# A chunked attention with two feed-forward layers on one core: another order of stores, preparation steps and low halves

## The chip, the cores and the metric

The kernel runs on one core of one Trainium2 chip. The metric is the device time of one execution in microseconds, the median of the runs. The core has TensorE (products; its weight loads are shown apart), VectorE (DVE), ScalarE (ACT), GpSimd (POOL) and SyncE (SP). In this kernel all DMAs are issued by SP, one after the other. Each engine takes its instructions in the order in which they are written; across engines only semaphores hold an instruction back.

## The reference

Attention within chunks of 64 tokens, 8 batches, 8 heads, 576 tokens, 64 columns a head; its output, 4608 tokens by 512, goes through two feed-forward layers with 2048 hidden columns:

```
scores = scale * q_c @ k_c^T ; attn = softmax(scores) ; x = attn @ v_c
h = x @ w_in1 ; g = h * sigmoid(1.702 h)               ; x = g @ w_out1
h = x @ w_in2 ; g = max(h, 0) + alpha * min(h, 0)      ; out = g @ w_out2
```

All arrays are float32 to the reader, but the weights arrive as 64-bit floats, so the kernel reads them as words and builds the 32-bit value from them ("decoding").

## The kernel before

**Precision.** A float32 factor is split into a high half (a cast by ScalarE to the type that TensorE multiplies fast) and a low half (the value minus the high half, a subtraction by VectorE or GpSimd). A product is three passes: high x high, low x high, high x low. Twelve matmuls of 128x512 are one such product of a tile.

**The plain stage.** The 4608 tokens are nine blocks of 512. The first five go through layer 1 in the plain form. For each block and each of 16 slices f of the hidden columns, `emit_h` makes 12 matmuls into `psH` (L652), ScalarE the activation and its high half, VectorE the low half `gs`, and `emit_y` 12 matmuls into `psY` (L682). One such pair is two *half slots*; there are 160. In the first block the weights are loaded, decoded (VectorE, L186 to L202) and split (`split_w`, high half by ScalarE L151, low half L154) as they are first needed.

Into the half slots a table puts everything else, as functions on a group of 128 tokens or on a step (`put(when, fn, g)`; `half_slot(k)` runs what is due). [...] Scores, maximum, exponential and normalization follow, and `att_PV` (L593) multiplies with the values that `load_v` brought. TensorE's `att_PV` reads what the fetch brings. For the first groups the buffer `off` is the one that also holds the scores `e`, read by the products of L558.

**Two kinds of preparation.** The last four blocks of layer 1, and all of layer 2, are computed by *pairs* of blocks with seven instead of eight products on quarters (Strassen and Winograd's scheme). It needs sums of quarters of the weights. For layer 1, 32 `fold` steps add them up on GpSimd from the weights that are in memory and store them (`wi<-fold`, `wo<-fold`). For layer 2, 32 *preparation steps* each load raw weights (`prep_load`, 2 DMAs), take the absolute value (`prep_abs`, ScalarE L183), decode (`prep_decode`, VectorE, 4 operations), make the sums (GpSimd, 4 operations, L293), cast two high halves (`hi`, ScalarE L283), subtract two low halves (GpSimd L285) and store all four (`wi<-g`, `wi<-u`, `wi<-sums`; `prep_store_a` and `prep_store_b`). 19 of these steps are in the plain stage, 13 in the first two pairs. A DMA that stores is queued by `send_later` and issued by `send_due` at the start of the next half slot, before that half slot's loads and swaps; the results `ysb` of a block are issued at once.

**The pairs.** A pair is four groups of 14 `h_item` (L903, six matmuls) and 7 `y_item` (L1051, twelve). A counter `clock` goes up by one for each `h_item` and by two for each `y_item`; `at(when, fn)` puts work at a value of it. Of the operands of the second product, GpSimd makes differences (`diff`, L984), ScalarE the high half (`op_hi`, L974) and VectorE the low half (`op_lo`, L979); in the first two pairs the loaded weights are split as well (`split_factor`, high L822, low L823 by GpSimd for `wi`, VectorE for `wo`). The first two pairs are layer 1's (`p < N1`), the other five layer 2's.

Of the kernel before, what the change touches and what calls it, by code (L numbers as in the profile page):

```python
# [36 lines left out]
TAU = (4, 10, 16, 22) + tuple(28 + 4 * i for i in range(28))  # L37
QK_T_AT = {4: 18, 5: 24}
QK_AT = {2: 3, 3: 9}
END = (4, 8)  # L40
PREP_AT = tuple(30 + 6 * i for i in range(19))
FOLD_AT = tuple(33 + 7 * i // 2 for i in range(32))
LATE_AT = (4, 20, 36, 52, 68, 84, 98)
# [26 lines left out]
def tile_chunk_attention_two_ffn(  # L70
# [185 lines left out]
    def send_later(**dma):  # L256
        waiting.append((half + 1, dma))

    def send_due():
        while waiting and waiting[0][0] <= half:  # L260
            nc.sync.dma_start(**waiting.pop(0)[1])

    def prep_store(step, lo, hi, ts):
        kind, j, m = step
        dst = wi2[j][:, lo:hi, m] if kind == "wi" else wo2[j // 2][:, lo:hi, j % 2, m]
        for a, t in enumerate(ts):
            (late.get("send") or send_later)(out=dst[:, :, a], in_=t)
# [40 lines left out]
    def fold(step):  # L308
# [17 lines left out]
        send_later(out=dst, in_=u)  # L326
# [80 lines left out]
    def off_copy(k):  # L407
        off_t[k] = off_p.tile([P, DW + PW], F32, tag="off", name="off")
# [9 lines left out]
    def off_fetch(k):  # L418
        t, o = ops_t[k], off_t.pop(k)
# [157 lines left out]
    def att_PV(g):  # L577
# [35 lines left out]
        if blk >= NPL:  # L613
            send_later(out=x1d[blk][:, :, i * P:(i + 1) * P], in_=xg)
# [7 lines left out]
    def split_x(j):  # L622
# [6 lines left out]
        for c in range(KT):  # L629
            nc.vector.tensor_tensor(  # L630
# [44 lines left out]
    def emit_y(n):  # L675
# [10 lines left out]
        if f == NF - 1:  # L686
            if j < NPL - 1:
                sbs = x_p.tile([P, 4, 512], F32, tag="x", name="ysb")
            for t, ps in enumerate(y_t.pop(j)):
# [8 lines left out]
                nc.sync.dma_start(out=x2d[j][:, t], in_=sb)  # L698
# [155 lines left out]
    def second_layer():  # L854
# [134 lines left out]
        def plan_group(p, gr, u):  # L989
# [6 lines left out]
            }.get((p, gr), (27, 30, 34, 36, 44, 46, 49))  # L996
            for i, nm, hi in zip(
# [7 lines left out]
                (p, gr), (24, 32, 29, 38)  # L1005
# [8 lines left out]
        def plan_late(p, u):  # L1014
            for when in LATE_AT:
# [9 lines left out]
        def plan_pair(p, u):  # L1025
# [154 lines left out]
    with tc.manual_schedule():  # L1180
# [72 lines left out]
        for i, g in enumerate(GROUP_ORDER):  # L1253
            t = TAU[i]
            if i < GPB:
                for fn, at in ((att_T, -3), (att_X, 1), (att_N, 2), (att_AT, 5), (att_PV, 6)):
                    if i > 0 or fn is not att_T:
                        put(t + at, fn, g)
                if i > 1:
                    put(QK_AT[i], partial(load_qkv, names="qk"), g)  # L1260
                if i == 0:
                    put(t, att_S_matmuls, g)
                put(t + 7, load_v, GROUP_ORDER[i + 1])
                continue
            pv = TAU[i + LAG] if i + LAG <= last else TAU[last] + END[i + LAG - last - 1]
            before = QK_T_AT.get(i, TAU[i - LAG] + 1)
            put(before - LEAD, load_nat, g)
            put(before, qk_T, g)
# [24 lines left out]
        for n in range(NPL * NF):  # L1293
# [72 lines left out]
        assert not between  # L1366
# [35 lines left out]
```

## Time and profile before

| what | us |
|---|---|
| median of 3 runs (1626.81 to 1630.45) | 1629.92 |
| the profiled execution, of which all rows here are | 1631.56 |
| its span, first to last instruction | 1629.8 |
| TensorE busy | 1550.8 |
| VectorE, ScalarE, GpSimd busy | 1218.5, 973.0, 739.8 |

The share of busy time is an average over stages. The plain stage lasts to about 543 us, the first two pairs to about 920 us, the rest is layer 2's pairs. The granted clock is the share of the full TensorE clock that the chip granted in a stretch: 1.00 is 2.4 GHz, 0.50 is 1.2 GHz.

### The profile page before, as it was taken

The numbers are of one execution on the slowest core, as the hardware profiler recorded it, in microseconds if no ns is written. First come the engines' busy times: TensorE is split into PE (matmuls) and PEld (weight loads), VectorE is DVE, ScalarE is ACT, GpSimd is POOL, SyncE is SP. The second block draws the span as 40 slices with busy tenths as digits, with TensorE's granted clock in tenths as the row PEclk, the third lists the DMA queues.
The fourth block names the chain that finished last, engine by engine and source line by source line (L and its number), as shares of the span: only waits on it lengthen the run. The fifth ranks groups of instructions, "written<-read, shape, count | busy, mean of one in ns | idle before, by whom it ended". The sixth has DMA issues, their size and how long they took to land.

```text
span 1629.8 us, 25569 instructions
## 1 busy us (share of the span) xinstructions
PE 1550.8 (95%) x9167; PEld 1293.0 (79%) x9169; DVE 1218.5 (75%) x1379; ACT 973.0 (60%) x1393; POOL 739.8 (45%) x637
## 2 busy tenths in 40 slices
PE   8998998999989988989899999999999999999998
PEld 5776786877778867767677788888888888999998
DVE  7988776676674547888778966887788778868767
ACT  6767665665564465656655665656565655656653
POOL 0003655646564187878878225332532342143330
PEclk9999999999999999999999999999999999999999
DMA  9914778787787264546645577669766966898984
GB/s 250 322 44 130 209 214 233 199 237 213 214 227 211 75 192 136 152 125 189 190 133 148 177 237 241 193 186 271 224 187 193 274 204 203 213 360 255 261 269 143
DMA packets 414223, 331.51 MB, mean 203 GB/s; under 512 B 138512, under 2 KB 348560, under 8 KB 414096
## 3 DMA queue, kind: packets, MB, share of 16 engines
q1 hardware_dynamic: 414096, 329.87, 69.2%
q8 instruction: 73, 1.20, 0.3%
q14 instruction: 54, 0.44, 0.1%
HBM read 251.67 MB, written 67.11 MB: 196 GB/s over the span
## 4 chain that ended last, share of the span: by engine, by line
PE 55%; DVE 9%; issue 5%; DMA 4%; POOL 4%; ACT 3%; SPq 1%; POOLq 0%; DVEq 0%; ACTq 0%
PE psYa L1051 14%; PE psHa L903 13%; PE psYb L1051 10%; PE psHb L903 9%; PE psY L682 5%; PE psH L652 4%; POOL u L293 1%; POOL u L285 1%; DMA wi2t<-wi 1%; DVE o L979 1%; DVE u L197 1%; DVE yacc L1089 1%; DMA w<-wo 1%; DVE xop L799 1%; DMA ops<-off 1%
## 5 line engine op out<-in xcount | busy, mean ns | idle before, releaser
L1051 PE MATMUL psYa<-o,w 128*128 128x512 f32 (+1 forms) x960 | 228.7, 386 | 24.0 <-DVE o L979 19.2
L652 PE MATMUL psH<-xs,wi 128*128 128x512 f32 x960 | 233.4, 393 | 5.2 <-ACT wi L151 3.6
L682 PE MATMUL psY<-gs,wo 128*128 128x512 f32 x912 | 230.4, 404 | 0.0
L1051 PEld LDWEIGHTS psYa<-o,w 128*128 128x128 f32 x960 | 180.9, 193 | 59.3 <-DVE o L979 23.5
L903 PE MATMUL psHa<-xop,wi2t 128*128 128x512 f32 (+1 forms) x960 | 218.3, 376 | 0.0
L652 PEld LDWEIGHTS psH<-xs,wi 128*128 128x128 f32 x960 | 180.5, 189 | 44.7 <-ACT wi L151 4.3
L984 POOL TENSOR_TENSOR tsum<-g,tsum 128x1024 f32<-128x1024 f32 (+1 forms) x54 | 143.0, 2649 | 158.3 <-DVE o L979 119.5
L682 PEld LDWEIGHTS psY<-gs,wo 128*128 128x128 f32 x912 | 174.1, 194 | 38.7 <-DVE gs L670 0.3
L903 PEld LDWEIGHTS psHa<-xop,wi2t 128*128 128x128 f32 x960 | 177.8, 189 | 28.9 <-ACT g L942 0.2
L984 POOL TENSOR_TENSOR tsum<-g,g 128x1024 f32<-128x1024 f32 (+1 forms) x27 | 61.6, 2283 | 288.4 <-DVE g L926 274.9
L903 PE MATMUL psHb<-xop,wi2t 128*128 128x512 f32 (+1 forms) x744 | 170.7, 377 | 8.4 <-POOL wi2t L823 7.3
L1051 PE MATMUL psYb<-o,w 128*128 128x512 f32 (+1 forms) x744 | 168.1, 374 | 0.0
L903 PEld LDWEIGHTS psHb<-xop,wi2t 128*128 128x128 f32 x744 | 136.9, 189 | 32.4 <-POOL wi2t L823 10.5
L918 ACT ACTIVATE neg<-g 128x1024 f32<-128x1024 f32 (+1 forms) x80 | 78.1, 976 | 127.2 <-DVE g L954 126.6
L1051 PEld LDWEIGHTS psYb<-o,w 128*128 128x128 f32 x744 | 136.9, 188 | 21.2 <-DVE yacc L1089 0.3
L979 DVE TENSOR_TENSOR o<-tsum,o 128x1024 fp32r<-128x1024 f32 (+1 forms) x61 | 72.2, 1184 | 65.0 <-ACT o L974 64.8
L670 DVE TENSOR_TENSOR gs<-g,gs 128x512 fp32r<-128x512 f32 x76 | 59.2, 780 | 75.8 <-ACT gs L665 75.8
L1089 DVE TENSOR_TENSOR yacc<-psYb,yacc 128x1024 f32<-128x1024 f32 (+1 forms) x73 | 83.0, 1137 | 42.3 <-PE psYb L1051 42.3
L1089 DVE TENSOR_TENSOR yacc<-psYa,yacc 128x1024 f32<-128x1024 f32 (+1 forms) x86 | 97.7, 1136 | 22.4 <-PE psYa L1051 22.4
L926 DVE SCALAR_TENSOR_TENSOR g<-g,neg 128x1024 f32<-128x1024 f32 (+1 forms) x80 | 100.3, 1254 | 8.5 <-ACT neg L920 8.5
L920 ACT ACTIVATE neg<-neg,minus_alpha 128x512 f32<-128x512 f32 (+1 forms) x160 | 100.2, 674 | 2.6
L979 DVE TENSOR_TENSOR o<-g,o 128x1024 fp32r<-128x1024 f32 (+1 forms) x62 | 96.6, 1558 | 5.1 <-ACT o L974 5.1
(179 smaller groups left out, 2931.7 us busy)
## 6 DMA issues: line engine op xcount, KB each, us to landing
w<-wo SPq DMA_DIRECT2D x140, 512.0 KB, 3.8
wi2t<-wi SPq DMA_DIRECT2D x210, 256.0 KB, 3.6
w<-wi SPq DMA_DIRECT2D x70, 256.0 KB, 3.7
w<-wo SPq DMA_DIRECT2D x56, 256.0 KB, 3.2
wi2t<-wi SPq DMA_DIRECT2D x74, 128.0 KB, 3.0
raw<-in_moe_w_in_dram SPq DMA_DIRECT2D x16, 512.0 KB, 8.3
raw<-in_moe_w_out_dram SPq DMA_DIRECT2D x16, 512.0 KB, 7.5
raw<-in_moe_w_in_dram SPq DMA_DIRECT2D x32, 256.0 KB, 3.8
```

The lines of the kernel that those rows point to most:

```text
L197: nc.vector.scalar_tensor_tensor(out=u, in0=hi, scalar=-0x40000000, in1=u, op0=ALU.bitwise_and, op1=ALU.bitwise_or,)
L652: nc.tensor.matmul(ps, w[:, a, c], xs[:, b, c], start=(i == 0), stop=(i == 3 * KT - 1))
L670: nc.vector.tensor_tensor(out=gs[:, 1], in0=g, in1=gs[:, 0].bitcast(F32), op=ALU.subtract)
L682: nc.tensor.matmul(y_t[j][t], w[:, a, t * P:(t + 1) * P], gs[:, b], start=(f == 0 and a + b == 0), stop=(f == NF - 1 and b == 1),)
L903: nc.tensor.matmul(ps, w[:, c, a], x[b][:, c], start=(k == 0 and i in (1, 2, 5)), stop=(k == 5 and i in (2, 3, 4)), skip_group_check=True,)
L918: nc.scalar.activation(out=neg, in_=src, func=AF.Relu, scale=-1.0)
L920: nc.scalar.activation(out=neg[:, jj], in_=neg[:, jj], func=AF.Copy, scale=minus_alpha[:, f + jj:f + jj + 1])
L926: nc.vector.scalar_tensor_tensor(out=g, in0=g, scalar=0.0, in1=neg, op0=ALU.max, op1=ALU.add)
L979: nc.vector.tensor_tensor(out=lo, in0=wide(homes[nm], n), in1=hi.bitcast(F32), op=ALU.subtract)
L984: eng.tensor_tensor(out=wide(homes[out], n), in0=wide(homes[x], n), in1=wide(homes[y], n), op=ALU.subtract,)
L1051: nc.tensor.matmul(ps[:, d, :n], w[:, jj, d, a], x[b][:, jj], start=(k == 0 and i in (1, 5, 2)), stop=(k == 5 and i in (3, 2, 4)), skip_gr ...
L1089: nc.vector.tensor_tensor(out=out_acc, in0=ps[:, :, :n], in1=acc, op=ALU.add)
```

## The change

In each half slot the stores that are due go out after the loads and swaps of that half slot (`send_due` behind the loop). Stores of a preparation step and of x1 are due in their own half slot, fold stores one later, the `ysb` stores are queued like the others (all but the last block's). Before a `hi` buffer is written again, stores of it that are still queued are issued. The fetch moves from 5 to 4 half slots behind the start of its group, the value load from 1 half slot after `att_PV` to the same one. The first two `off` tiles share the buffer `raw2`, which then serves the preparation's loads. 22 instead of 19 steps are in the plain stage, every 5 half slots from 28 instead of every 6 from 30; 10 instead of 13 are in the pairs, at other values of the counter, and within a step the load comes one later, the decoding one earlier (with the absolute value), the second cast two later. In the first block 14 low halves of weights, and 3 of the second block's input, are GpSimd's. Some other entries of the tables move by one or two.

```diff
@@
-TAU = (4, 10, 16, 22) + tuple(28 + 4 * i for i in range(28))
-QK_T_AT = {4: 18, 5: 24}
...
-END = (4, 8)
-PREP_AT = tuple(30 + 6 * i for i in range(19))
...
-LATE_AT = (4, 20, 36, 52, 68, 84, 98)
...
+QK_T_AT = (17, 23)
...
+LO_POOL_O = (0, 0, 0, 1, 0, 0, 1, 0, 1, 1, 1, 1, 1, 0, 0, 1)
...
+XS_POOL = (0, 1, 1, 1)
...
+PREP_STAGE = (0, 3, 4, 6, 9)
+LATE_STAGE = (1, 5, 5, 8, 13)
...
+OFF_AT = (3, 3, 4)
+V_AT = 0
...
+LATE_0 = (12, 34, 52, 74, 92)
+LATE_1 = (10, 30, 48, 70, 90)
@@
-    def send_later(**dma):
-        waiting.append((half + 1, dma))
-
-    def send_due():
-        while waiting and waiting[0][0] <= half:
-            nc.sync.dma_start(**waiting.pop(0)[1])
+    def send_later(after=1, **dma):
+        waiting.append((half + after, dma))
+
+    def send_due(all_of=None):
+        for item in [w for w in waiting if (w[0] <= half if all_of is None else w[1]["in_"] is all_of)]:
+            waiting.remove(item)
+            nc.sync.dma_start(**item[1])
...
         hi = hi[:, :n]
+        while sent_hi:
+            send_due(sent_hi.pop())
         nc.scalar.copy(hi, src)
         hi = hi.bitcast(F32)
+        sent_hi.append(hi)
...
     def off_copy(k):
-        off_t[k] = off_p.tile([P, DW + PW], F32, tag="off", name="off")
+        if k < GPB + LAG:
+            if k == GPB:
+                off_t[k + 1] = raw_p.tile([P, 2, DW], F32, tag="raw2", name="off")
+            off_t[k] = off_t[GPB + 1][:, k - GPB]
+        else:
+            off_t[k] = off_p.tile([P, DW + PW], F32, tag="off", name="off")
...
-                nc.sync.dma_start(out=x2d[j][:, t], in_=sb)
+                if j == NPL - 1:
+                    nc.sync.dma_start(out=x2d[j][:, t], in_=sb)
+                else:
+                    send_later(YSB_SEND + t // 2, out=x2d[j][:, t], in_=sb)
...
-                        (0, prep_load), (5, prep_abs), (6, prep_decode), (8, prep_store_a), (11, prep_store_b),
+                        *zip(LATE_STAGE, (prep_load, prep_abs, prep_decode, prep_store_a, prep_store_b)),
...
-                send_due()
                 for fn, x in between.pop(k, []):
                     fn(x)
+                send_due()
...
-                        split_w(*key, nc.vector)
+                        split_w(*key, nc.gpsimd if (LO_POOL_O if key[0] == "wo" else LO_POOL_I)[key[2]] else nc.vector)
```

SP, fourth swap of the plain stage, before: send, raw load, three stores, value load, fetch (`fold`, `g`, `u` and `sums` are what the stores read; `x2` counts equal rows).

```order
L416 DMA ops_1684<-ops_1684 32x768 x2
L250 DMA raw2_1801<-in_moe2_w_in_dram 128x2x128 x2
L261 DMA wi2_0_129<-g_141 128x3x128
L261 DMA wi2_0_129<-u_1687 128x3x128
L261 DMA wi1_0_117<-fold_1804 896x1x128
L365 DMA v_1831<-in_v_dram 128x8x64
L422 DMA ops_1684<-off_1734 32x768 x2
```

The same swap after, with the rows next to it.

```order
L284 DMA wi1_0_117<-fold_1688 896x1x128
L284 DMA wi2_0_129<-g_141 128x3x128
L284 DMA wi2_0_129<-u_1616 128x3x128
L449 DMA ops_1685<-ops_1685 32x768 x2
L393 DMA v_1805<-in_v_dram 128x8x64
L455 DMA ops_1685<-off_1745 32x768 x2
L284 DMA wi1_0_117<-fold_1811 896x1x128
L284 DMA wi2_0_129<-g_141 128x4x128
L284 DMA wi2_0_129<-sums_1734 128x4x128
```

Three stores that stood between send and fetch stand before the send or behind the fetch. In other swaps the two stores of a preparation step still stand between, as in the next one:

```order
L449 DMA ops_1840<-ops_1840 32x768 x2
L284 DMA wi2_0_129<-g_141 128x3x128
L284 DMA wi2_0_129<-u_1809 128x3x128
L393 DMA v_1958<-in_v_dram 128x8x64
L455 DMA ops_1840<-off_1895 32x768 x2
```

ScalarE in the first block, around the first `off_copy`, before (`ops<-psX` copies the transposes of group 7, `wo` and `wi` are high halves of weights).

```order
L662 ACTIVATE g_141<-psH_1097 128x512
L183 ACTIVATE u_1126<-raw_666 128x512
L183 ACTIVATE u_1127<-raw_787 128x512
L669 CAST gs_1110<-g_141 128x512
L446 COPY ops_1152<-psX_525 128x512 x2
L410 COPY off_1163<-ops_1123 128x512
L151 CAST wo_1179<-u_1068 128x512
```

And after.

```order
L695 ACTIVATE g_141<-psH_1100 128x512
L443 COPY off_1126<-ops_1097 128x512
L205 ACTIVATE u_1128<-raw_666 128x512
L205 ACTIVATE u_1129<-raw_787 128x512
L702 CAST gs_1113<-g_141 128x512
L479 COPY ops_1154<-psX_525 128x512 x2
L173 CAST wo_1181<-u_1068 128x512
```

The copy stands one half slot earlier, before the copies of group 7's transposes.

ScalarE in the first pair, one preparation step, before: absolute value, first cast `hi`, second cast `hi`.

```order
L183 ACTIVATE u<-raw_5740 128x512
L822 CAST w_5823<-w_5823 128x4x128
L958 ACTIVATE g_6077<-g_6077 128x1024
L974 CAST o_6083<-g_6078 128x1024
L822 CAST w_5738<-w_5738 128x2x128 x2
L283 CAST hi<-u 128x384
L974 CAST o_6085<-tsum 128x1024
L822 CAST w_5819<-w_5819 128x4x128
L958 ACTIVATE g_6076<-g_6076 128x1024
L822 CAST wi2t<-wi2t 128x2x128
L283 CAST hi<-u 128x512
```

And a step of the first pair after.

```order
L205 ACTIVATE u<-raw_5809 128x512
L858 CAST wi2t<-wi2t 128x2x128
L978 ACTIVATE g_6143<-psHa 128x1024
L858 CAST w_5885<-w_5885 128x4x128
L310 CAST hi<-u 128x384
L858 CAST wi2t<-wi2t 128x2x128
L1010 CAST o_6152<-g_6140 128x1024
L858 CAST wi2t<-wi2t 128x2x128
L858 CAST w_5886<-w_5886 128x4x128
L987 COPY g_6140<-psHa 128x1024
L1010 CAST op3h<-tsum 128x1024
L310 CAST hi<-u 128x512
```

Between the two casts stand six other rows instead of four.

## Rows read from the trace of the kernel before

**Rows 1.** The page's engine table: busy us (share of the span) xinstructions.

```profile
PE 1550.8 (95%) x9167; PEld 1293.0 (79%) x9169; DVE 1218.5 (75%) x1379; ACT 973.0 (60%) x1393; POOL 739.8 (45%) x637
```

**Rows 2.** Stretches: length, busy PE, PEld, DVE, ACT, POOL, granted clock, DMA share, GB/s.

```profile
25.00:130.00 105.00, 100.34 (x786) 75.81 (x787) 96.34 (x187) 72.68 (x120) 4.18 (x4) 0.98 0.62 187
130.00:490.00 360.00, 332.97 (x2895) 271.00 (x2894) 253.49 (x396) 222.91 (x339) 200.97 (x285) 0.96 0.76 212
...
570.00:920.00 350.00, 314.41 (x1292) 248.65 (x1291) 272.18 (x239) 208.92 (x325) 270.24 (x214) 0.96 0.54 158
920.00:1600.00 680.00, 679.86 (x3270) 595.93 (x3269) 522.28 (x458) 407.49 (x505) 236.75 (x93) 1.00 0.77 233
```

**Rows 3.** TensorE's waits, whole span: us in total, times, longest.

```profile
PE psX L593 <- DMA ops<-off: 25.3, 7, 6.3
PE psYa L1051 <- DVE o L979: 19.2, 10, 4.8
PE psHb L903 <- POOL wi2t L823: 7.3, 5, 2.2
PE psH L652 <- ACT wi L151: 3.6, 2, 1.8
```

**Rows 4.** Timeline of TensorE, 84 to 122 us: start, us, instruction [idle before, releaser].

```profile
86.41 1.04 PE L438 MATMUL psX<-ident,qk 128*128 128x128 f32 x8
...
95.78 4.61 PE L652 MATMUL psH<-xs,wi 128*128 128x512 f32 x12 [1.80 <-ACT wi L151]
...
104.30 2.88 PE L652 MATMUL psH<-xs,wi 128*128 128x512 f32 x12
```

**Rows 5.** Stretch behind the first of these stops.

```profile
96.40:99.80 3.40, 3.40 (x10) 2.62 (x9) 3.40 (x9) 2.05 (x5) 0.00 (x0) 0.50 0.51 138
```

**Rows 6.** Timeline of ScalarE, 84 to 122 us.

```profile
86.12 0.60 ACT L662 ACTIVATE g<-psH 128x512 f32<-128x512 f32 x1
...
116.52 0.62 ACT L410 COPY off<-ops 128x512 f32<-128x512 f32 x1 [4.88 <-PE psX L558]
```

**Rows 7.** GpSimd by line, 130 to 490: count, busy, mean ns, idle before.

```profile
L154 POOL TENSOR_TENSOR wo<-u,wo 128x512 fp32r<-128x512 f32 x4 | 5.5, 1376 | 36.5 <-ACT wo L151 36.5
```

**Rows 8.** VectorE by line, 25 to 130 us.

```profile
L154 DVE TENSOR_TENSOR wi<-u,wi 128x512 fp32r<-128x512 f32 x16 | 10.9, 684 | 2.2 <-ACT wi L151 2.2
```

**Rows 9.** VectorE by line, 570 to 920 us.

```profile
L823 DVE TENSOR_TENSOR w<-w 128x512 fp32r<-128x512 f32 x49 | 52.3, 1067 | 19.5 <-ACT w L822 19.1
```

**Rows 10.** Timeline of SP, 150.5 to 164 us: start and us of issuing.

```profile
151.25 1.21 SPq L416 DMA_DIRECT2D ops<-ops  x2
...
157.03 0.37 SPq L261 DMA_DIRECT2D wi<-u  x1
161.16 0.59 SPq L261 DMA_DIRECT2D wi<-fold  x1
...
162.50 1.84 SPq L422 DMA_DIRECT2D ops<-off  x2
```

**Rows 11.** DMA issues, 130 to 490 us: count, KB each, median us to landing.

```profile
ops<-ops SPq DMA_DIRECT2D x52, 96.0 KB, 3.1
ops<-off SPq DMA_DIRECT2D x52, 96.0 KB, 3.6
```

**Rows 12.** Timeline of SP, 249 to 259 us.

```profile
250.20 4.62 SPq L698 DMA_DIRECT2D x<-ysb  x4
...
256.98 1.88 SPq L422 DMA_DIRECT2D ops<-off  x2
```

**Rows 13.** ScalarE by line, 570 to 920 us.

```profile
L283 ACT CAST hi<-u 128x384 fp32r<-128x384 f32 (+1 forms) x26 | 14.7, 566 | 51.7 <-DVE u L202 35.0 <-POOL u L285 16.4 <-issue 0.3
```

**Rows 14.** GpSimd by line, 570 to 920 us.

```profile
L293 POOL TENSOR_TENSOR u<-u 128x128 f32<-128x128 f32 x52 | 38.2, 755 | 23.9 <-DVE u L202 14.5 <-issue 8.4
L285 POOL TENSOR_TENSOR u<-u,hi 128x384 fp32r<-128x384 f32 (+1 forms) x26 | 37.2, 1429 | 1.1
```

**Rows 15.** SP's waits, 130 to 490 us: total, times, longest.

```profile
SPq L261 <- POOL sums L293: 18.3, 10, 4.0
```

More of the change, by code (lines that the diff above doesn't have):

```diff
@@ L36 @@
 LEAD = 3
-TAU = (4, 10, 16, 22) + tuple(28 + 4 * i for i in range(28))
-QK_T_AT = {4: 18, 5: 24}
-QK_AT = {2: 3, 3: 9}
-END = (4, 8)
-PREP_AT = tuple(30 + 6 * i for i in range(19))
-FOLD_AT = tuple(33 + 7 * i // 2 for i in range(32))
-LATE_AT = (4, 20, 36, 52, 68, 84, 98)
+TAU = (4, 10, 16, 22, 28, 32, 36, 40, 44, 48, 52, 56, 60, 64, 68, 72, 76, 80, 84, 88, 92, 96, 100, 104, 108, 112, 116, 120, 124, 128, 132, 136)
+QK_T_AT = (17, 23)
+OFF_FIRST = (1, 2, 4)
+QK_4 = (4, 9)
+ATT_FIRST = (-3, 1, 2, 5, 6, 7)
+LO_POOL_O = (0, 0, 0, 1, 0, 0, 1, 0, 1, 1, 1, 1, 1, 0, 0, 1)
+LO_POOL_I = (0, 0, 0, 1, 0, 1, 0, 0, 0, 0, 1, 0, 1, 1, 1, 0)
+XS_POOL = (0, 1, 1, 1)
+END = (6, 9)
+PREP_AT = (28, 33, 38, 43, 48, 53, 58, 63, 68, 73, 78, 83, 88, 93, 98, 103, 108, 113, 118, 123, 128, 133)
+FOLD_AT = (33, 36, 40, 44, 47, 50, 54, 57, 61, 63, 68, 71, 75, 78, 82, 85, 89, 93, 96, 100, 104, 107, 110, 113, 116, 119, 123, 127, 131, 134, 138, 141)
+FOLD_SEND = 1
+X1_SEND = 0
+YSB_SEND = 0
+PREP_STAGE = (0, 3, 4, 6, 9)
+LATE_STAGE = (1, 5, 5, 8, 13)
+ATT_AT = (1, 1, 2, 2)
+OFF_AT = (3, 3, 4)
+V_AT = 0
+D_AT = 1
+SUMS_AT = (43, 47, 72, 74)
+X_HI_AT = (3, 8, 20, 24, 33, 37, 46)
+FIRST_LOAD = 28
+GROUP_OP = (27, 30, 34, 36, 44, 46, 47)
+GROUP_SUM = (24, 32, 29, 38)
+PREP_SEND = (0, 0)
+LATE_0 = (12, 34, 52, 74, 92)
+LATE_1 = (10, 30, 48, 70, 90)
 PAIRS_1 = (512, 512)
@@ L266, in prep_store @@
         for a, t in enumerate(ts):
-            (late.get("send") or send_later)(out=dst[:, :, a], in_=t)
+            (late.get("send") or partial(send_later, PREP_SEND[a]))(out=dst[:, :, a], in_=t)
     def prep_abs(step):
@@ L297, in prep_store_a @@
         sums = (
-            late["sums"].rearrange("p (q f) -> p q f", q=4) if late
+            late["sums"].rearrange("p (q f) -> p q f", q=4) if "sums" in late
             else dec_p.tile([P, 4, P], F32, tag="u", name="sums")
@@ L325, in fold @@
         dst = wi1[j][:, :, m] if kind == "wi" else wo1[j // 2][:, :, j % 2, m]
-        send_later(out=dst, in_=u)
+        send_later(FOLD_SEND, out=dst, in_=u)
     def spans(t0, n):
@@ L613, in att_PV @@
         if blk >= NPL:
-            send_later(out=x1d[blk][:, :, i * P:(i + 1) * P], in_=xg)
+            send_later(X1_SEND, out=x1d[blk][:, :, i * P:(i + 1) * P], in_=xg)
     following = dict(zip(GROUP_ORDER[:GPB], GROUP_ORDER[1:]))
@@ L629, in split_x @@
         for c in range(KT):
-            nc.vector.tensor_tensor(
+            (nc.gpsimd if j == 1 and XS_POOL[c] else nc.vector).tensor_tensor(
                 out=xs[:, 1, c], in0=x[:, c], in1=xs[:, 0, c].bitcast(F32), op=ALU.subtract
@@ L995, in plan_group @@
                 (NP - 1, NGR - 2): (27, 30, 34, 33, 44, 42, 40),
-            }.get((p, gr), (27, 30, 34, 36, 44, 46, 49))
+            }.get((p, gr), GROUP_OP if p < N1 else (27, 30, 34, 36, 44, 46, 49))
             for i, nm, hi in zip(
@@ L1014, in plan_late @@
         def plan_late(p, u):
-            for when in LATE_AT:
+            for when in (LATE_0, LATE_1)[p]:
                 if unprepared:
@@ L1255, in tile_chunk_attention_two_ffn @@
             if i < GPB:
[L1256 removed]
+                for fn, at in zip((att_T, att_X, att_N, att_AT, att_PV), ATT_FIRST):
                     if i > 0 or fn is not att_T:
@@ L1365, in tile_chunk_attention_two_ffn @@
                 more_homes()
-        assert not between
+        assert not between and not waiting
         emit_y(NPL * NF - 1)
```

33 lines of the change are left out of this document (16 added, 17 removed).

## The prediction

> **What bounds the kernel now.** I read the page's engine table first: TensorE is busy 1550.8 us, 95% of the span [rows 1]. A change can only give back what TensorE does not do, 79 us, and what its clock withholds. Next comes the sum by stretch, cut where the program's stages change [rows 2]. From 920 to 1600 us, the second layer's pairs, TensorE is busy for 679.86 of 680 us at a granted clock of 1.00, so nothing can be won there. From 25 to 130 us it stands for 4.7 us, from 130 to 490 us (attention and preparation) for 27.0 us, from 570 to 920 us (the first layer's two pairs) for 35.6 us. In the last two the granted clock is 0.96. Then the list of TensorE's waits says for whom [rows 3]: 25.3 us in 7 stops for the fetch `ops<-off`, 19.2 us in 10 stops for VectorE's low part `o`, 7.3 us in 5 stops for GpSimd's low half `wi2t`, 3.6 us in 2 stops for ScalarE's `wi`. Those are the places to follow, one by one.
>
> The clock is a second price on each stop. After the stop of 1.80 us at 95.78 us, 12 matmuls took 4.61 us; 12 others at 104.30 us took 2.88 us [rows 4]. In between the granted clock reads 0.50, the lower of the two levels, 1.2 GHz [rows 5]. So a stop of about 2 us costs some 1.7 us more. A mean of 0.96 over 360 us is 14.4 us withheld, over 350 us 14.0 us; where TensorE stands anyway it costs nothing, so I take 11 us and 12 us. With the idle time: 38 us in the plain stage and 48 us in the pairs are at stake, and 4.7 + 1.7 = 6.4 us in the first block, 92 us in all.
>
> **Part 1, the first block.** The second copy `off` stands on ScalarE for 4.88 us before it starts, at 116.52 us, until TensorE's products of L558 have read `e` [rows 6]: `off` and `e` share one buffer. So does the first. Queued behind each are the casts of the next weights, and TensorE waits for them 1.80 us, twice [rows 3, 4]. After the change the first two copies share the buffer `raw2`. The first then has to wait only for the transposes of group 7, one half slot on; by the present times they end at 87.45 us [rows 4], 0.7 us after the activation ahead of the copy [rows 6]. The second waits for nothing. Saved: 2 x 1.80 + 1.7 = 5.3 us; I take 5, between 0 (the new wait as long as the old one) and the 6.4.
>
> The 14 weight halves and 3 input halves that go to GpSimd cost 1.376 us each there [rows 7] against 0.684 us on VectorE [rows 8]. GpSimd is busy 4.18 of 105 us in this stretch and VectorE 96.3 [rows 2], so the work lands on an idle engine, and it frees 17 x 0.684 = 11.6 us of the fullest. A product reads a low half from its fifth matmul on, a third of 2.88 us after its start [rows 4], so 0.7 us more hides. I cost it at nothing; without that cover it is 17 x 0.69 = 11.8 us.
>
> The Trainium skill, "SBUF — State Buffer", section "SBUF: two separate sides", speaks against this part: GpSimd and a VectorE operation with two SBUF inputs share one port pair under an exclusive lock, and the second of them fully blocks. The trace leans that way: a low half of 128x512 takes VectorE 0.684 us where GpSimd is nearly idle [rows 8] and 1.067 us in the pairs, where GpSimd is busy 270 of 350 us [rows 2, 9]. What it would do here is the second rival below.
>
> **Part 2, the plain stage.** At 151.25 us SP issues the sends `ops<-ops`, and only at 162.50 us the fetch [rows 10]. Between them the store `wi<-u` is issued at 157.03 us and `wi<-fold` at 161.16 us, each once GpSimd has its data; SP issues in order, so the fetch stands behind them, lands 3.6 us after its issue in the median [rows 11], and TensorE stands for 6.3 us, the longest of the seven [rows 3]. At 250.20 us four stores `x<-ysb` hold SP for 4.62 us and the fetch goes out at 256.98 us [rows 12]. The change takes the fetch one half slot forward. A half slot holds one batch of 12 matmuls, 2.88 us [rows 4], and a share of attention's small ones, so about 3 us. It also puts the fold stores, the x1 stores and the `ysb` stores behind the fetch of their half slot. At the first place this gives 3 us and the 4.1 us from 157.03 to 161.16; at the second 3 + 4.6 us. The other five stops are shorter (25.3 - 6.3 us over six, this one among them). By this arithmetic every one of them goes, 38 us. What is late next: the fetch may not overwrite what the send reads, and must wait for the send to land, 3.1 us after its issue [rows 11], one half slot: there is no more to gain by going earlier. And the preparation's own stores, which wait for GpSimd, still stand between send and fetch in many groups, as the order after shows.
>
> Three more preparation steps go into this stage. Each has 6 DMAs; 18 x 0.65 us (the pair of sends takes 1.21 us [rows 10]) is 12 us of SP's issue, 0.4 us per group of four half slots. GpSimd gets at most 3 x 5.9 = 18 us more (the price of a step in the pairs, below) on 201 of 360 us [rows 2]: hidden. VectorE has room too, 253 of 360. The forced flush before a reuse of `hi` finds nothing left to send, since the stores go out in their own half slot. The value loads move into the half slot whose product frees the buffer, which costs SP a short wait. For all this I keep a quarter and take 28 us of the 38; the ends are a loss of 12 us (the added issue all on the path) and 38.
>
> **Part 3, the pairs.** ScalarE's cast `hi<-u` of a preparation step stands idle 51.7 us in 26 casts, 35.0 us for VectorE's decoding and 16.4 us for GpSimd's sums [rows 13]: 2.7 us before the first cast of each of the 13 steps, 1.3 us before the second. Behind it are the operand casts whose low parts TensorE waits for [rows 3]. The pairs after 920 us, which have neither such steps nor the splitting of loaded weights, show no stop at all [rows 2]. So I divide the stage by its steps: (35.6 + 12) / 13 = 3.7 us each.
>
> Three steps go: 11 us. The other ten are spread: decoding one clock unit earlier, the second cast two later. A unit is half of 12 matmuls, about 1.4 us by the same 2.88 us. The first cast has three units after decoding instead of two, which leaves 2.7 - 1.4 = 1.3 us; the second has two units, 2.8 us, more than before, which covers its 1.3. ScalarE's wait falls by two thirds. If TensorE's stops fell with it, ten steps would give 24 us; I take 14, because GpSimd still does its own burst (4 x 0.755 + 2 x 1.429 = 5.9 us a step [rows 14]) ahead of the halves that cost 7.3 us [rows 3], and because decoding now stands in the same unit as the ScalarE operation it reads, so VectorE may wait. Ends: 10 steps keep their 3.7 us, or lose all 37. Part 3 is 25 us, between 0 and 48. The shifted times of loads and sums in the pairs I cost at nothing; they lie beside the same work.
>
> **Sum.** 5 + 28 + 25 = 58 us off the profiled execution's 1631.6 us: 1573.6. The median of the runs, 1629.9, lies 1.6 us under it, so 1572; I say 1573.
>
> **The rivals.** *The swaps stay late* (17%). A group of four half slots has, counted in the code, about 15.9 issues after (15.1 before), 10.3 us of 12; the stores of `sums` alone made it wait 18.3 us [rows 15], and some still precede the fetch. For: SP has little spare time. Against: the fetch has a half slot more. The plain stage then gives only 5 us: 1630 - 5 - 5 - 25 = 1595.
>
> *GpSimd holds VectorE in the first block* (8%). By lock, each of the 17 halves could hold VectorE 1.376 us: 96.3 - 11.6 + 23.4 = 108.1 us in a stretch of 105. The block gains nothing and lengthens by 3 us: 1573 + 5 + 3 = 1581. Against: VectorE meets a GpSimd operation only part of the time. The Trainium skill's rule on the port pair (same page) is this case in full.
>
> *The steps in the pairs only get fewer* (15%): the spread changes nothing, each keeps its 3.7 us. 1573 + 14 = 1587. For: GpSimd's burst is as long as before.
>
> *Slower* (6%): SP becomes the bound in the plain stage. It is slower than before if the stage loses more than the 30 us of the other parts, 1.1 us in each of about 28 groups on top of today's 1.4 us of loss. SP would have to wait over 12 + 2.5 - 10.3 = 4.2 us in every group, more than the longest single wait for `sums`, 4.0 us, against 18.3 / 28 = 0.7 us now [rows 15]. Then about 1638.
>
> That the change does not what it says (3%): the fetch still stands behind as many waiting stores; no change. Against: the order after shows it directly behind the value load.
>
> **How the numbers follow.** The forecast has 51%, with a range of its own from 1552 to 1592. The range for 8 in 10 takes in the first three rivals, and downward part of the case that nearly all 92 us go (1538), and above 1595 some room for a loss inside the first rival: 1550 to 1612. Faster or slower counts from 0.2%, 3 us, about what a measurement of this kernel can tell from no change. Faster: 0.51 + 0.17 + 0.08 + 0.15 = 0.91; same: 0.03; slower: 0.06.
>
> **What would show it.** Right: no wait of TensorE for `ops<-off` above 1 us, none for `wi` of 1.8 us in the first block, the fetch's issue at least 6 us ahead of its reader; in the pairs ten casts `hi<-u` of each kind with under 20 us of idle in all, and TensorE's waits for `o` under 10 us. Wrong: SP's waits for GpSimd above 50 us with the fetch still last to land; VectorE's low halves in the first block at 1 us and new waits there; or stops in the pairs with the same 2.7 us of idle before the first cast.

## The result, and the profile after

The changed kernel takes 1591.19 us (median of 4 runs, 1588.90 to 1593.78) against 1630.18 us before: a ratio of 0.9761, 95% interval [0.9733, 0.9788], so 39 us faster. The forecast was 1573, with 1550 to 1612: the sign and the range hold, the gain is 18 us smaller than forecast.

The page's engine table after (columns as in [rows 1]):

```profile
PE 1540.2 (97%) x9167; PEld 1286.7 (81%) x9169; DVE 1235.9 (78%) x1362; ACT 974.0 (61%) x1393; POOL 770.7 (48%) x654
```

The span is 1592.0 us instead of 1629.8. TensorE's idle time fell from 79.0 to 51.8 us; its busy time fell by 10.6 us with the same 9167 instructions, so these ran at the higher clock more often. The stretches of [rows 2], after (the first two pairs now end 37 us earlier):

```profile
25.00:130.00 105.00, 96.17 (x698) 71.24 (x696) 93.28 (x170) 70.93 (x117) 30.97 (x17) 0.94 0.62 191
130.00:490.00 360.00, 347.66 (x3106) 283.33 (x3105) 279.43 (x426) 241.41 (x367) 228.06 (x315) 0.99 0.82 228
...
570.00:890.00 320.00, 300.23 (x1268) 240.03 (x1268) 280.57 (x228) 198.95 (x304) 248.45 (x187) 0.98 0.54 159
890.00:1560.00 670.00, 669.85 (x3221) 587.18 (x3220) 512.36 (x448) 399.81 (x494) 233.59 (x92) 1.00 0.79 234
```

For each stretch I add the idle time and the withheld clock (one minus the granted clock, times the length). First block: 4.7 + 2.1 = 6.8 us before, 8.8 + 6.3 = 15.1 after, 8 worse. Plain stage: 41.4 before, 12.3 + 3.6 = 15.9 after, 25 better. Pairs: 35.6 + 14.0 = 49.6 before, 19.8 + 6.4 = 26.2 after, 23 better. That is 40 us in sum (clock withheld while TensorE stands is counted twice) for the 37.8 of the span.

These stretches end at fixed times, so before and after they do not hold quite the same work. Three products of TensorE bound the stages by the program: the first of the second block, of the first pair and of the third pair, before and then after.

```profile
134.23 2.88 PE L652 MATMUL psH<-xs,wi 128*128 128x512 f32 x12
562.42 2.88 PE L903 MATMUL psHa<-xop,w 128*128 128x512 f32 x12
905.02 2.88 PE L903 MATMUL psHa<-xop,wi2t 128*128 128x512 f32 x12
```

```profile
143.87 2.88 PE L685 MATMUL psH<-xs,wi 128*128 128x512 f32 x12
549.18 2.88 PE L939 MATMUL psHa<-xop,w 128*128 128x512 f32 x12
867.61 2.88 PE L939 MATMUL psHa<-xop,wi2t 128*128 128x512 f32 x12
```

The first block's own first product starts at 25.42 us before and 26.81 after. So the first block is 8.2 us longer, the four other blocks of the plain stage 22.9 shorter, the first two pairs 24.2 shorter, and the rest 0.4 shorter; the remaining 1.4 us lie ahead of the first block. The forecast had 5 better, 28 better and 25 better. The first block has the wrong sign, and it is 13 of the 20 us by which the profiled execution misses the sum. Below, "by the products" means these lengths, each from one profiled execution.

TensorE's waits after, as [rows 3]:

```profile
PE psYa L1087 <- DVE o L1015: 9.7, 7, 2.7
PE psH L685 <- POOL wi L176: 8.5, 3, 5.0
PE psX L626 <- DMA ops<-off: 7.1, 4, 2.6
PE psHb L939 <- POOL w L859: 4.0, 3, 2.0
```

The fetch `ops<-off` (the two DMAs that SP issues behind the sends `ops<-ops`; `att_PV` reads what they bring) is down from 25.3 to 7.1 us, `o` from 19.2 to 9.7, and ScalarE's `wi` is gone. New are three stops for low halves `wi` that GpSimd now makes. GpSimd's timeline in the first block (start, us, instruction, [idle before, releaser]):

```profile
39.87 1.29 POOL L176 TENSOR_TENSOR wi<-u,wi 128x512 fp32r<-128x512 f32 x1 [20.27 <-DMA raw<-in_moe_w_out_dram]
...
112.19 1.63 POOL L176 TENSOR_TENSOR wo<-u,wo 128x512 fp32r<-128x512 f32 x1 [4.22 <-ACT wo L173]
...
120.02 5.68 POOL L176 TENSOR_TENSOR wo<-u,wo 128x512 fp32r<-128x512 f32 x1 [3.49 <-ACT wo L173]
125.66 1.44 POOL L176 TENSOR_TENSOR wi<-u,wi 128x512 fp32r<-128x512 f32 x1
```

The same subtraction takes 1.29 to 1.63 us, but 5.68 us at 120.02 (and 5.35 us at 52.01). What VectorE does meanwhile:

```profile
119.81 0.68 DVE L703 TENSOR_TENSOR gs<-g,gs 128x512 fp32r<-128x512 f32 x1
120.41 0.75 DVE L208 TENSOR_SCALAR u<-u 128x512 f32<-128x512 f32 x2
121.08 0.75 DVE L213 TENSOR_SCALAR u<-u 128x512 int32<-128x512 int32 x2
121.75 1.28 DVE L219 SCALAR_TENSOR_TENSOR u<-raw,u 128x512 int32<-128x512 int32 x2
122.96 1.28 DVE L224 SCALAR_TENSOR_TENSOR u<-raw,u 128x512 int32<-128x512 int32 x2
124.16 0.42 DVE L208 TENSOR_SCALAR u<-u 128x512 f32<-128x512 f32 x1
124.61 1.37 DVE L213 TENSOR_SCALAR u<-u 128x512 int32<-128x512 int32 x1
```

Behind `gs` it runs nine decoding operations, one close behind the other, until 124.58 us. GpSimd's half ends 1.12 us after that first gap, and the next VectorE operation now takes 1.37 us instead of 0.42. The other held half ends 1.13 us after the run of VectorE that lies beside it, which ends at 56.23 us. TensorE's wait that follows, and the stretch behind it:

```profile
127.16 3.78 PE L685 MATMUL psH<-xs,wi 128*128 128x512 f32 x8 [5.03 <-POOL wi L176]
```

```profile
127.20:132.20 5.00, 5.00 (x56) 3.77 (x60) 3.55 (x6) 1.21 (x2) 0.00 (x0) 0.50 0.00 0
```

The product needs `wi`, which stood behind the held `wo` on GpSimd: 5.03 us of stop, and then 5 us at the lower level, 1.2 GHz.

The clock did not fall behind the first of the three stops in every execution. The run "Only the fetch late" below has the same first block, with the same hold of 5.35 us. The same eight matmuls behind that stop, in the changed kernel and then in that run:

```profile
58.63 3.78 PE L685 MATMUL psH<-xs,wi 128*128 128x512 f32 x8 [2.59 <-POOL wi L176]
```

```profile
57.59 2.11 PE L685 MATMUL psH<-xs,wi 128*128 128x512 f32 x8 [2.59 <-POOL wi L176]
```

There the first block takes 113.8 us instead of 117.1, and 2.6 us of that lie behind this stop. So some 3 of the 8.2 us belong to this one execution and its clock; why it fell in one and not in the other stays open.

### The profile page after: what moved, and what is told of

Its sections match the earlier page's. It is cut to its first block, busy times and chain, and to the rows that moved or that the text cites. A ratio compares the mean times of both kernels' runs of the same rounds, so it can differ in the third digit from the quotient of the medians.

```text
span 1592.0 us, 25635 instructions
## 1 busy us (share of the span) xinstructions
PE 1540.2 (97%) x9167; PEld 1286.7 (81%) x9169; DVE 1235.9 (78%) x1362; ACT 974.0 (61%) x1393; POOL 770.7 (48%) x654
## 4 chain that ended last, share of the span: by engine, by line
PE 59%; DVE 12%; DMA 6%; issue 4%; ACT 3%; POOL 2%; SPq 1%; POOLq 0%; DVEq 0%; ACTq 0%
PE psYa L1087 15%; PE psHa L939 14%; PE psYb L1087 10%; PE psHb L939 9%; PE psY L715 5%; PE psH L685 5%; DVE yacc L1125 2%; DVE o L1015 2%; DVE w L859 2%; DMA wi2t<-wi 1%; DVE u L219 1%; DMA raw<-in_moe_w_in_dram 1%; DVE u L208 1%; DVE g L990 1%; DVE u L213 1%
## 5 line engine op out<-in xcount | busy, mean ns | idle before, releaser
L1020 POOL TENSOR_TENSOR tsum<-g,tsum 128x1024 f32<-128x1024 f32 (+1 forms) x54 | 146.8, 2719 | 167.4 <-DVE o L1015 130.9
L715 PE MATMUL psY<-gs,wo 128*128 128x512 f32 x912 | 224.5, 396 | 0.2 <-DVE gs L703 0.2
L939 PE MATMUL psHa<-xop,wi2t 128*128 128x512 f32 (+1 forms) x984 | 222.6, 375 | 0.5 <-ACT g L978 0.5
L939 PEld LDWEIGHTS psHa<-xop,wi2t 128*128 128x128 f32 x984 | 181.7, 188 | 29.6 <-ACT g L978 1.0
L715 PEld LDWEIGHTS psY<-gs,wo 128*128 128x128 f32 x912 | 170.0, 189 | 37.4 <-DVE gs L703 0.7
L939 PE MATMUL psHb<-xop,wi2t 128*128 128x512 f32 (+1 forms) x720 | 163.5, 375 | 2.0 <-POOL wi2t L859 2.0
L939 PEld LDWEIGHTS psHb<-xop,wi2t 128*128 128x128 f32 x720 | 132.5, 188 | 23.7 <-POOL wi2t L859 3.1
L703 DVE TENSOR_TENSOR gs<-g,gs 128x512 fp32r<-128x512 f32 x76 | 62.9, 828 | 78.5 <-ACT gs L698 76.0
L1015 DVE TENSOR_TENSOR o<-g,o 128x1024 fp32r<-128x1024 f32 (+1 forms) x62 | 101.0, 1628 | 0.3 <-ACT o L1010 0.3
```

Of the source, the lines that this page charges most:

```text
L703: nc.vector.tensor_tensor(out=gs[:, 1], in0=g, in1=gs[:, 0].bitcast(F32), op=ALU.subtract)
L715: nc.tensor.matmul(y_t[j][t], w[:, a, t * P:(t + 1) * P], gs[:, b], start=(f == 0 and a + b == 0), stop=(f == NF - 1 and b == 1),)
L939: nc.tensor.matmul(ps, w[:, c, a], x[b][:, c], start=(k == 0 and i in (1, 2, 5)), stop=(k == 5 and i in (2, 3, 4)), skip_group_check=True,)
L1015: nc.vector.tensor_tensor(out=lo, in0=wide(homes[nm], n), in1=hi.bitcast(F32), op=ALU.subtract)
L1020: eng.tensor_tensor(out=wide(homes[out], n), in0=wide(homes[x], n), in1=wide(homes[y], n), op=ALU.subtract,)
```

## The experiments

Theory A: a low half on GpSimd is held while VectorE runs its decoding, and two such halves, with the clock, are the loss in the first block. Rivals: VectorE was too full anyway (B); GpSimd is simply slower (C). For the swaps and the pairs the question is which part of the edit gave the gain. Ratios are to the kernel before, timed on the same chip in the same session; 0.001 is 1.6 us. The changed kernel has 0.9761.

**All 14 halves of weights back on VectorE.**

```diff
-LO_POOL_O = (0, 0, 0, 1, 0, 0, 1, 0, 1, 1, 1, 1, 1, 0, 0, 1)
-LO_POOL_I = (0, 0, 0, 1, 0, 1, 0, 0, 0, 0, 1, 0, 1, 1, 1, 0)
+LO_POOL_O = (0,) * 16
+LO_POOL_I = (0,) * 16
```

> The changed kernel with the 14 low halves of weights back on VectorE (the three of the second block's input stay on GpSimd). In the changed kernel TensorE waits 8.5 us in three stops for GpSimd's `wi` halves, and the granted clock over 25 to 130 us is 0.94, 6.3 us withheld. Theory A (a low half on GpSimd is held while VectorE runs its decoding): the three stops and their clock go, VectorE gets 14 x 0.69 = 9.7 us more on 93.3 of 105, some of it shows: 9 us less than 1591, about 1582. Rival B (VectorE was the fuller engine, so the halves are better off on GpSimd even with the stops): VectorE at 103 of 105 us makes TensorE wait for decoding instead, no gain or a loss, 1590 to 1600.

Measured: 1583.31 us, ratio 0.9721 [0.9698, 0.9745], 6.5 us by the ratios where A expected 9. The first block:

```profile
25.00:130.00 105.00, 102.18 (x799) 76.98 (x800) 100.79 (x192) 74.29 (x124) 4.19 (x4) 1.00 0.64 193
```

TensorE stands for 2.8 us at the full clock, although VectorE is busy 100.8 of 105. Rival B falls. Without these halves the block's loss is 2.8 us against 6.8 before, and by the products it is 3.2 us shorter than before (105.6 against 108.8 us). That is what the rest of the change is worth in this block, less than the forecast's 5 for the `off` copies, which were not tried alone.

**Only the four halves of the two held slots back.**

```diff
-LO_POOL_O = (0, 0, 0, 1, 0, 0, 1, 0, 1, 1, 1, 1, 1, 0, 0, 1)
-LO_POOL_I = (0, 0, 0, 1, 0, 1, 0, 0, 0, 0, 1, 0, 1, 1, 1, 0)
+LO_POOL_O = (0, 0, 0, 0, 0, 0, 1, 0, 1, 1, 1, 1, 0, 0, 0, 1)
+LO_POOL_I = (0, 0, 0, 1, 0, 0, 0, 0, 0, 0, 1, 0, 1, 1, 0, 0)
```

> The changed kernel with only four low halves back on VectorE: `wo` 3 and `wi` 5, `wo` 12 and `wi` 14, the two slots in which the `wo` half took GpSimd 5.35 and 5.68 us where the other six before 130 us took 1.61 to 1.63. Theory A (hold): the stops at 58.6 and 127.2 us (2.6 and 5.0 us) go with their two half-clock stretches of 6.8 us each (about 3 us lost in each), the remaining ten halves keep taking 1.3 to 1.6 us: 12 to 13 us less, 1579. Rival C (GpSimd's halves are late because two on one engine take 2.9 us where VectorE's take 1.4): the stop of 0.9 us at 115.1 shows what this is worth; the other slots with two halves get worse stops as the program is earlier, 3 to 6 us less, 1586.

Measured: 1582.14 us, 0.9709 [0.9685, 0.9734]. Windows, and GpSimd by line in the first block:

```profile
25.00:130.00 105.00, 103.47 (x806) 77.40 (x803) 99.66 (x184) 75.38 (x126) 17.32 (x13) 0.99 0.63 192
130.00:490.00 360.00, 345.43 (x3071) 281.00 (x3070) 274.13 (x419) 241.19 (x369) 240.19 (x332) 1.00 0.85 236
```

```profile
L176 POOL TENSOR_TENSOR wo<-u,wo 128x512 fp32r<-128x512 f32 x5 | 8.1, 1622 | 27.6 <-ACT wo L173 27.6
```

The other halves stay at 1.62 us in the mean and cost one stop of 0.9 us. The whole loss of the first block sat in two slots, as A says; the block itself gained what was expected, 15.1 to 2.6 us (12.4 by the products), but the rest of the plain stage became 2.4 us longer by the products, and by the ratios 8.5 us remain.

**Two small operations more on VectorE, in the same two slots.** Nothing is taken away.

```diff
+    pause = const.tile([P, 8], F32, tag="pause", name="pause")
+    nc.vector.memset(pause, 1.0)
...
+                    if n in (4, 13):
+                        for _ in range(2): nc.vector.reciprocal(out=pause, in_=pause)
```

> The changed kernel with two small operations more on VectorE (reciprocals of a 128x8 tile in place, about 0.2 us each) ahead of the decoding in the same two slots; nothing is moved to another engine. In the changed kernel VectorE's first decoding operation starts 0.40 us after the `wo` half there, and 0.46 us or later in the slots where the half is not held. Theory A (hold, decided by which of the two engines comes first): GpSimd comes first, its `wo` halves take 1.6 us, VectorE's first operation behind it 1.1 instead of 0.42, the stops of 2.6 and 5.0 us go: 10 to 13 us less, about 1580, although work was only added. Rival C (GpSimd is too slow or starts too late): nothing changes or 0.8 us more, 1591 to 1592.

Measured: 1586.98 us, 0.9743 [0.9719, 0.9767]. Timelines of GpSimd and of VectorE at the second of these slots, then windows:

```profile
114.58 1.62 POOL L176 TENSOR_TENSOR wo<-u,wo 128x512 fp32r<-128x512 f32 x1 [3.49 <-ACT wo L173]
```

```profile
114.97 0.43 DVE L1346 RECIPROCAL pause<-pause 128x8 f32<-128x8 f32 x2
115.32 2.57 DVE L208 TENSOR_SCALAR u<-u 128x512 f32<-128x512 f32 x2
```

```profile
25.00:130.00 105.00, 102.80 (x806) 76.56 (x799) 100.40 (x183) 74.40 (x123) 23.40 (x17) 0.99 0.69 198
130.00:490.00 360.00, 345.39 (x3022) 281.11 (x3021) 273.23 (x420) 239.93 (x365) 234.91 (x325) 0.98 0.85 232
```

This is the run that shows the mechanism: the half takes 1.62 instead of 5.68 us (in the other slot 1.61 instead of 5.35) with every instruction of the changed kernel still in its place, and now VectorE is held, 2.57 us for two operations that take 0.75. The first block loses 3.3 us where it lost 15.1. C falls. Of these 12 us only some 3 reach the end (the intervals of the two kernels overlap): the plain stage, which is now entered earlier, loses 14.6 + 7.2 us against 15.9. That part of the expectation missed.

**Stores, fetch and value load as before.**

```diff
-OFF_AT = (3, 3, 4)
-V_AT = 0
+OFF_AT = (3, 3, 5)
+V_AT = 1
...
+                send_due()
                 for fn, x in between.pop(k, []):
                     fn(x)
-                send_due()
```

> The changed kernel with the order of stores and swaps as before: what is due is sent at the start of a half slot, the fetch 5 instead of 4 half slots behind its group's start, the value load one half slot later; the steps, their spread and the first block stay. The plain stage went from 27.0 to 12.3 us of TensorE's idle time and from a clock of 0.96 to 0.99. Theory D (the gain there is that of the fetch, the prediction's 28 us): the stops for `ops<-off` come back with their clock, 23 us more, 1614. Rival E (the gain comes from other entries that moved, or is less since 22 steps were planned around it): 5 us more, 1596. If the denser steps need the new order, over 1620.

Measured: 1620.24 us, 0.9945 [0.9924, 0.9966]. The plain stage, and SP's waits in it (us in total, times, longest):

```profile
130.00:490.00 360.00, 328.58 (x2883) 266.84 (x2881) 253.25 (x401) 223.99 (x342) 210.65 (x301) 0.97 0.78 217
```

```profile
SPq L284 <- POOL sums L321: 23.3, 15, 3.9
SPq L284 <- POOL fold L321: 20.1, 14, 3.4
```

The three edits together are worth 30 us by the ratios, about the prediction's 28 for the stage; E falls. By the products 26.6 us of it lie between the second block and the pairs. TensorE's stops from 130 to 490 us are now 14.9 us in nine for the fetch, 5.7 us in one for the values `v` and 2.6 us in one for VectorE. In the changed kernel SP waits less for the same stores:

```profile
SPq L284 <- POOL fold L321: 12.9, 13, 2.4
...
SPq L284 <- POOL sums L321: 6.3, 10, 1.6
```

**Only the stores ahead of the swaps** (`send_due()` at the start of the half slot, as in the diff above).

> The changed kernel with only the order within a half slot as before: stores that are due go out at its start, ahead of its loads and swaps (so a store queued in one half slot is sent in the next, before the swap). The fetch stays at 4 half slots behind its group's start. Undoing this, the fetch and the value load together gave 1620. Theory D1 (stores that wait for GpSimd or TensorE hold the fetch, the 4.1 and 4.6 us of the prediction's two places): most of the 29 us comes back, 1610 to 1618. Rival D2 (it is the fetch's earlier half slot that counts, 3 us at each stop): 1593 to 1600.

Measured: 1596.08 us, 0.9792 [0.9774, 0.9809]: 5 us, though the intervals of the two kernels overlap. D1 falls; the time is that of D2, but the next run takes D2 away as well.

**Only the fetch late.**

```diff
-OFF_AT = (3, 3, 4)
+OFF_AT = (3, 3, 5)
```

> The changed kernel with only the fetch back at 5 half slots behind its group's start; stores stay behind the swaps, the value load stays early. Undoing order, fetch and value load together cost 29 us, the order alone 5. Theory D2 (the fetch's half slot counts: 3 us and the clock at most of the 28 groups whose fetch now lands just in time): 12 to 20 us more, 1603 to 1611. Rival D3 (the parts only cost together: either of the two keeps the fetch early enough): 5 us more or less, 1596.

Measured: 1589.71 us, 0.9752 [0.9738, 0.9766]: no loss, and none by the products in the plain stage either. So undoing the order or the fetch's half slot alone costs 5 us or nothing, and the three edits together 30. D3, that either of the two keeps the fetch early enough, fits this but is not shown: the value load was not undone alone, nor the two without it. That nine of the eleven stops with all three undone are for the fetch, and one for the values, speaks for D3.

**The old times within a step of the pairs.**

```diff
-LATE_STAGE = (1, 5, 5, 8, 13)
+LATE_STAGE = (0, 5, 6, 8, 11)
```

> The changed kernel with the times within a preparation step of the pairs as before (load, absolute value, decoding, first and second stores at 0, 5, 6, 8, 11 instead of 1, 5, 5, 8, 13); still ten such steps. From 570 to 890 us TensorE is idle 19.8 us in the changed kernel. Theory F (the prediction's: spreading gives 14 us of the 25): the 16.8 us of ScalarE's idle time before the casts `hi` rise to about 40 (4 a step), TensorE's stops for `o` return: 1605. Rival G (the steps only got fewer; the spread changes nothing): 1591, within 3.

Measured: 1595.61 us, 0.9787 [0.9773, 0.9800]; about 4 us (5.1 by the products, all in the pairs), not told apart from the changed kernel by the intervals, and much nearer to G than to F's 1605. ScalarE's casts `hi` from 570 to 890 us, in this run and then in the changed kernel:

```profile
L310 ACT CAST hi<-u 128x512 fp32r<-128x512 f32 (+1 forms) x19 | 10.8, 569 | 34.5 <-DVE u L224 17.4 <-POOL u L313 14.7 <-DMA wo<-hi 2.4
```

```profile
L310 ACT CAST hi<-u 128x512 fp32r<-128x512 f32 (+1 forms) x19 | 10.8, 567 | 16.8 <-DVE u L224 16.1 <-POOL u L313 0.7
```

The spread halves ScalarE's idle time, yet 18 us of it are worth 4 us: most was not on TensorE's path.

**13 steps in the pairs, and 8.**

```diff
-LATE_0 = (12, 34, 52, 74, 92)
-LATE_1 = (10, 30, 48, 70, 90)
+PREP_AT = tuple(30 + 6 * i for i in range(19))
+LATE_0 = (4, 20, 36, 52, 68, 84, 98)
+LATE_1 = (4, 20, 36, 52, 68, 84, 98)
```

> The changed kernel with 19 preparation steps in the plain stage (every 6 half slots from 30) and 13 in the pairs, at the counter values of before; the spread within a step stays new. Theory F (a step in the pairs costs, with the new spread, what is left: (19.8 + 5.8) / 10 = 2.6 us; the prediction took 3.7): three more cost 8 to 11 us, the plain stage gives back at most 3: 1597 to 1602. Rival H (the number does not matter, the gain in the pairs is from spread and table alone): 1588 to 1591.

```diff
+PREP_AT = tuple(28 + 5 * i for i in range(24))
+LATE_0 = (12, 36, 62, 88)
+LATE_1 = (10, 34, 60, 86)
```

> The changed kernel with 24 steps in the plain stage (every 5 half slots from 28, the last at 143) and 8 in the pairs (four in each). If a step in the pairs costs 2.6 us and the plain stage takes two more for nothing: 5 us less, 1586. If SyncE or GpSimd in the plain stage is full by now (the stops for `ops<-off` grow): 1591 or more. What the runs of 13, 10 and 8 steps give together is the price of a step.

Measured: 1607.73 us, 0.9857 [0.9844, 0.9871] with 13; 1580.28 us, 0.9683 [0.9668, 0.9698] with 8. Windows of the two:

```profile
130.00:490.00 360.00, 353.64 (x3115) 288.18 (x3115) 266.28 (x414) 237.07 (x361) 214.61 (x303) 1.00 0.80 222
570.00:890.00 320.00, 291.36 (x1204) 232.49 (x1204) 268.53 (x228) 191.44 (x297) 252.31 (x197) 0.96 0.55 159
```

```profile
570.00:890.00 320.00, 307.07 (x1322) 248.52 (x1323) 283.61 (x230) 203.31 (x308) 236.03 (x173) 0.99 0.54 160
```

From 13 to 10 steps the time falls by 15.6 us, from 10 to 8 by 12.7: 5 to 6 us a step, more than either run was expected to show. The prediction had 3.7. By the products the first two pairs are 21.1 us longer with 13 and 12.4 us shorter with 8, 6 to 7 us a step; the plain stage behind the first block is 3.8 us shorter with 19 steps and 1.3 us shorter with 24. H, that the number does not matter, falls as far as number and place can be told apart: each of the two runs also moved the remaining steps to other values of the counter, and the same number at other values was not tried.

**The two faster edits together** (four halves on VectorE, 24 and 8 steps).

> Two versions that were faster put together: the four low halves of the two held slots back on VectorE (1582.1, -8 us), 24 steps in the plain stage and 8 in the pairs (1580.3, -13 by the ratios). They touch different stages, so if the gains add: 1571. If what the first block gives is lost again in the plain stage (later stops for `ops<-off`, as in the run with the two small operations): 1576 to 1580.

Measured: 1575.97 us, 0.9664 [0.9651, 0.9678]: clearly faster than before and than the changed kernel, the fastest version found; against the 8 steps alone (0.9683) the intervals overlap.

```profile
25.00:130.00 105.00, 102.62 (x802) 77.66 (x803) 99.95 (x186) 75.48 (x125) 17.75 (x14) 1.00 0.65 194
130.00:490.00 360.00, 347.30 (x3063) 282.42 (x3062) 273.73 (x415) 237.15 (x362) 232.33 (x325) 0.98 0.85 235
```

The gains do not add: the plain stage loses 12.7 + 7.2 us, more than with the four halves alone (14.6 us, at a clock of 1.00). By the products the pairs, too, gain only 8.9 us here, against 12.4 with the 8 steps alone.

**26 and 28 steps in the plain stage**, 6 and 4 in the pairs, with the same four halves on VectorE.

```diff
+PREP_AT = tuple(28 + 23 * i // 5 for i in range(26))
+LATE_0 = (12, 46, 80)
+LATE_1 = (10, 44, 78)
```

> The same four halves on VectorE, 26 steps in the plain stage (every 4.6 half slots from 28, the last at 143) and 6 in the pairs. The runs with 13, 10 and 8 steps in the pairs give about 5 us a step: 10 us less than with 8, 1561, as far as the pairs have that much left (12.9 us idle of 320 with 8). Rival (the plain stage pays: steps nearer to each other hold SyncE, VectorE and the `hi` buffer): 1571 or more.

> The same with 28 steps in the plain stage (every 4.25 half slots) and 4 in the pairs. By 5 us a step 1551, by what the pairs had left with 8 steps (12.9 us) at best 1560. If the plain stage is full, it turns here: more than with 26 steps. I expect it within 5 us of the 26.

Measured: 1611.19 us, 0.9892 [0.9874, 0.9910], and 1617.21 us, 0.9915 [0.9903, 0.9927]. It turns between 24 and 26: with 26 the plain stage behind the first block is 37.8 us longer than with 24, by the products, and the pairs are 4.2 us shorter. The plain stage with 26, TensorE's largest wait over the whole span, and two of SP's in that stage:

```profile
130.00:490.00 360.00, 322.31 (x2838) 259.99 (x2837) 266.73 (x392) 218.21 (x336) 221.87 (x303) 0.97 0.78 219
```

```profile
PE psX L626 <- DMA ops<-off: 20.0, 13, 4.4
```

```profile
SPq L284 <- ACT g L310: 11.8, 7, 3.1
SPq L272 <- DVE u L224: 9.1, 5, 4.6
```

SP now waits to issue a step's raw load until the decoding of the step before has read `raw2`, and to store a high half (`g`) until ScalarE has made it; the fetch stands behind them again, and its stops return. In the changed kernel these two waits are 2.2 us for `g` and none for that decoding. Neither size was expected; the first run's rival, that the plain stage pays, had the direction. Whether the number or the closer spacing does it was not tried.

## Why the prediction was right, and where it was not

**Part 1, the `off` copies: right in cause.** The 3.6 us for ScalarE's `wi` are gone, and with the halves on VectorE the block gains 3.2 us by the products, of the 5.

**Part 1, the 17 halves "cost at nothing": the step that failed.** It weighed engines that were idle over the stretch and the 0.69 us by which a half is longer. The size was wrong, since a half could take 5.7 us, and so was the cover: `wi` was queued behind `wo` on GpSimd. The bound of 11.8 us was near the 13 us measured (from 5 better to 8 worse) by luck: all 17 halves were to cost 0.69 us each, but two cost nearly everything, and some 3 us belong to one execution's clock. The 1.7 us of clock for a stop were no fixed price either: the same stop of 2.59 us cost 2.6 us more in one execution than in the other. The second rival came closest and had it the wrong way round: it let GpSimd hold VectorE, for 1.376 us a time, and gave 1581. VectorE was held too (its ten remaining `wi` halves took 0.872 us in the mean, not the 0.684 of [rows 8]), but what cost was that it held GpSimd. The sign of being wrong came in part: their mean stayed under 1 us, but there are new waits in the first block.

The Trainium skill, "SBUF — State Buffer", section "SBUF: two separate sides", states the rule both ways: of a GpSimd operation and a VectorE operation that takes the shared port pair, whichever starts first has it, and the other blocks. The trace agrees that one of the two engines blocks, with 5.68 us for GpSimd and 1.37 us for VectorE at 120 us. On who goes first it differs: by the profile the held half starts at 120.02 us, ahead of the nine decoding operations that start from 120.41 us on, and yet it ends behind them.

**Part 2: right in size, not in its split.** 22.9 us by the products against 28, and 30 with the three edits undone. The two places behaved as told: at the first, the send and the fetch that stood 11.25 us apart [rows 10] are now 2.5 us apart; at the second, the fetch of 253.29 us goes out ahead of the fold and x1 stores.

```profile
161.71 1.23 SPq L449 DMA_DIRECT2D ops<-ops  x2
163.04 0.54 SPq L393 DMA_DIRECT2D v<-in_v_dram  x1
164.25 1.14 SPq L455 DMA_DIRECT2D ops<-off  x2
```

But the prediction added 3 us for the fetch's half slot to 4.1 or 4.6 for the order; alone, the one is worth nothing and the other some 5 us. Its two signs of being right were not met: stops for the fetch of up to 2.6 us remain, where none above 1 us was to be left, and this fetch is issued 3.6 us ahead of its reader at 167.89 us, not 6, about what it takes to land (3.1 us in the median). "Hidden" for three more steps held up to 24 and no further.

**Part 3: right in size, for the other reason.** 24.2 us by the products against 25. The spread was to give 14 and gave 5; three steps fewer, at their values of the counter, were to give 11 and gave 21. That the two errors cancel is luck. The signs held (16.8 us of idle time before the casts, 9.7 us for `o`) and still did not tell the parts apart: ScalarE's idle time was no measure of TensorE's. That is the rival "only get fewer" in its cause, at a higher price per step.

**Sum.** 13 us too much in part 1, 5 in part 2, 1 in part 3, and the 1.4 us ahead of the first block: the 20 us between the sum's 58 and the 37.8 of the profiled executions. By the medians it is 18 us, from 1573 to 1591.

## What to carry to other kernels

Moving work to an idle engine is not free because its mean load is low: look at which operations of the other engine run in the same microseconds, and at what is queued behind the moved one. Two edits against the same wait may cover for each other, so undo them together as well as one by one before giving either a price. An engine's idle time counts only where the bound engine waits for it. Measure a stage between two instructions of the program, not between two times: that shows where a gain won early is partly taken back by the next stage, here by 2 to 7 us of some 12.

## What the hardware showed that was not expected

GpSimd was kept out not by one VectorE operation but by a whole run of them, 0.42 to 0.68 us each: it got in at the first small gap (0.03 us, at 124.58 us) and finished 1.12 us later. Two operations of 0.2 us on a 128x8 tile at the run's head were enough to let it in, and shortened it from 5.68 to 1.62 us. The section on the chip says that across engines only semaphores hold an instruction back; here a half on GpSimd and an operation on VectorE were held by each other, after they had started by the profile.
